# Weight narrowing in three separately emitted steps, outer products and token sums on GpSimd, and a new order of attention slots and loads, in a fused sketch-attention and gated-FFN kernel

## The chip, the cores and the metric

The kernel runs on one core of one Trainium2 chip. The metric is device time in microseconds (us). The core has five engines that run their own instruction streams: TensorE (PE, matmuls; its weight loads are shown as PEld), VectorE (DVE), ScalarE (ACT), GpSimd (POOL) and SyncE (SP, which here issues DMAs). They wait for one another through semaphores.

## The reference

Attention with a polynomial sketch: q and k are projected by two 8 x 32 sketches, and the outer product of the two projections (64 features) replaces the softmax kernel. Its output, laid out as 4352 tokens by 128, goes through a gated feed-forward layer. All in float32 for 4 batches, 4 heads, 1088 tokens, head width 32, and a hidden width of 1536:

```python
def phi(x):
    a = np.einsum('rd,bhsd->bhsr', S1, x)
    b = np.einsum('rd,bhsd->bhsr', S2, x)
    return np.einsum('bhsi,bhsj->bhsij', a, b).reshape(*x.shape[:-1], r * r)
q_p, k_p = (phi(q), phi(k))
kv = np.einsum('bhsf,bhsd->bhfd', k_p, v)
z = np.sum(k_p, axis=2)
num = np.einsum('bhsf,bhfd->bhsd', q_p, kv)
den = np.einsum('bhsf,bhf->bhs', q_p, z)[..., None] + 1e-06
attn = num / den
x = attn.transpose(0, 2, 1, 3).reshape(B * S, H * D)
gate = 1.0 / (1.0 + np.exp(-(x @ w_gate)))
return gate * (x @ w_val) @ w_out
```

The sketches and the three weight matrices arrive as float64 bits (pairs of 32-bit words), and the kernel turns them into float32 itself.

## The kernel before

**Feed-forward.** The 4352 tokens are cut into eight chunks of 512 and one of 256 (`tok_chk`). For each chunk there are 12 "waves", one for each 128-wide tile j of the hidden width (six in the last chunk, two tiles each). `w1` (from L287) issues a wave: two 128x512 matmuls into a `wave` PSUM tile (L300), a sigmoid on ACT (`sg`, L308), and a closure `glu` that multiplies value by gate on DVE (`g`, L313). `w2` (L252) accumulates `g` times the output weights into `moeout` (L258), two waves later. There are 102 waves.

**Attention.** For each batch: DVE transposes k (`turn_k`, tile `kT`, L356) and, in two chunks, q (`turn_q`, `qT`, L368). `kps` (L380) projects k, and DVE turns the result back (`kab`, L390). `outer` (L399) forms the products `kp` of one head. `kv` (L459) accumulates kp times v, and for batches 1 to 3 adds one matmul on `zs` (L471), the sum over tokens that `sum_z` (L493 to L497) makes of kp in four additions. `ab` (L422) projects q by both sketches into `aps` and `bps`; ACT copies aps to `asb` (L432) and DVE multiplies bps by it into `qp` (L441). Then `ndt` turns the copied kv (`kvd`, L482) on PE into `ndps`, from which DVE copies the denominators' weights `zb` (L514) and the numerators' weights `nd` (L516). `den` (L523) and its inversion (L534 to L541), `num` (L558) and the division into `xT` (L568) follow, for each q chunk. `xT` is what the waves read.

**The order.** Emission order sets the order on each engine; nothing reorders it. `slot(group, waves)` issues one attention group and then so many waves, so that PE always finds both kinds of work; the list of slots is written out by hand at the end of the function. PSUM has two `wave` tiles (shared by aps), one `two` tile (kps, bps, nps) and one `one` tile (kvz, ndps, dps), so a group can wait for the reader of the one before. dps takes the place of ndps and so waits for the copies of both zb and nd.

**Narrowing.** `narrow` turns a 128x3x128 tile of float64 bits, hidden tile j of all three matrices, into `w_sb`: `cap` (clamp of the high words, L94, DVE, reading every other word), two steps for `head` (L99, L103, DVE), `tail` (L107, ACT, low words), a square of cap (L108, ACT), an integer add of head and tail (L109, POOL), and the last step, a compare and multiply into `w_sb` (L113, DVE). During the first chunk wave j emits all but the last step for tile j+3 and then the last step of tile j+1, ahead of its matmuls. Tiles 0, 1 and 2 are narrowed ahead of the first wave. The pairs of tiles are loaded by `load_w`, four ahead.

**Loads.** SP issues all of them: the sketch rows, k and q of batch 0 in two halves each (288 and 256 KB), v, the first four weight pairs, then batch 1.

Of the kernel before, what the change touches and what calls it, by code (L numbers as in the profile page):

```python
# [14 lines left out]
MUL = ALU.mult  # L15
# [5 lines left out]
def kernel(  # L21
# [34 lines left out]
    sbN = ctx.enter_context(tc.tile_pool(name="sbN", bufs=4))  # L56
# [17 lines left out]
    q_chk = [(0, 9), (9, TP - 9)]  # L74
# [6 lines left out]
    def narrow(out, bits):  # L81
# [7 lines left out]
        def tmp(dt, tag):  # L89
            return sbN.tile([P, 3, P], dt, tag=tag, name=tag)[:, :n, :m]  # L90


        cap, head, tail = tmp(I32, "cap"), tmp(I32, "head"), tmp(I32, "tail")
        nc.vector.tensor_scalar(  # L94
            out=cap.bitcast(F32), in0=hi.bitcast(F32), scalar1=122880.0, scalar2=-122880.0,
            op0=ALU.min, op1=ALU.max,
        )

        nc.vector.tensor_scalar(  # L99
# [6 lines left out]

        nc.scalar.activation(out=tail, in_=lo, func=ACTF.Copy, scale=2.0**-29)  # L107
        nc.scalar.activation(out=cap.bitcast(F32), in_=cap.bitcast(F32), func=ACTF.Square)  # L108
        nc.gpsimd.tensor_tensor(out=head, in0=head, in1=tail, op=ALU.add)  # L109


        def last():
            nc.vector.scalar_tensor_tensor(  # L113
                out=out, in0=cap.bitcast(F32), scalar=1.265625 * 2.0**-30, in1=head.bitcast(F32),
                op0=ALU.is_ge, op1=MUL,
            )

        return last
# [49 lines left out]


    def load_rows(src, b, tag, parts=((0, T),)):  # L170
        t = ld.tile([P, T, D], F32, tag=tag, name=tag)
        for t0, t1 in parts:
            nc.sync.dma_start(
                out=t[:, t0:t1, :],
                in_=bass.AP(
                    tensor=src.tensor,
                    offset=src[b, 0].offset + t0 * D,
                    ap=[[T * D, P], [1, (t1 - t0) * D]],
                ),
            )  # L180
        return t
# [59 lines left out]

    zb = []
    for n in range(2):
        t = const.tile([P, H, 32], F32, tag=f"zb{n}", name=f"zb{n}")
        nc.gpsimd.memset(t, 0.0)
        zb.append(t)
# [40 lines left out]
    def w1():  # L287
# [107 lines left out]
    def outer(b, h, j0=0, j1=NJK):  # L395
# [3 lines left out]
        nc.vector.tensor_tensor(  # L399
# [89 lines left out]
    def sum_z(b):  # L489
# [3 lines left out]
        nc.vector.tensor_tensor(out=z4, in0=kp[:, :, 1:5], in1=kp[:, :, 5:9], op=ALU.add)  # L493
        nc.vector.tensor_tensor(out=z4[:, :, :2], in0=z4[:, :, :2], in1=z4[:, :, 2:], op=ALU.add)
        zs = sbA.tile([P, H, F], F32, tag="zs", name="zs")
        nc.vector.tensor_tensor(out=zs, in0=z4[:, :, 0], in1=z4[:, :, 1], op=ALU.add)
        nc.vector.tensor_tensor(out=zs[:64], in0=zs[:64], in1=kp[:64, :, 0], op=ALU.add)  # L497
        return zs

    def ndt(b):  # L500
# [15 lines left out]
        nc.vector.tensor_copy(out=ND[b], in_=ndps[:, 0, :P])  # L516
# [61 lines left out]
    turn_k(0, halves)  # L578
# [5 lines left out]
    for h in range(H):  # L584
        outer(0, h, 0, 5)
    kv(0, [1, 2, 3, 4])
    for h in range(H):
        outer(0, h, 5, NJK)
# [22 lines left out]
    turn_q(1, 0)  # L611
    slot(lambda: r_group((1, 0, 0), (0, 1, 1)), 1)
    slot(lambda: den(0, 1)(), 1)
    slot(lambda: num(0, 1)(), 1)
    turn_k(1)
    slot(lambda: kps(1), 1)

    for b in range(1, B):
        more = b + 1 < B

        few = b == 1
        load_batch(b + 1)
        if b == 1:
            for h in range(H):
                outer(b, h)
        turn_q(b, 1)
        slot(lambda: r_group((b, 1, 0), (b, 0, 0)), 1)
        zs = sum_z(b)
        slot(lambda: kv(b, [1, 2, 3, 4], zs), 1 if few else 2)
        slot(lambda: r_group((b, 0, 1), (b, 1, 0)), 1)  # L630
        turn_k(b + 1)
        slot(lambda: kv(b, [5, 6, 7, 8, 0], zs), 1 if few else 2)
        slot(lambda: r_group((b, 1, 1), (b, 0, 1)), 1)
        turn_q(b + 1, 0)
        if more:
            slot(lambda: kps(b + 1), 1 if few else 2)
            outer(b + 1, 0)
        slot(lambda: r_group((b + 1, 0, 0) if more else None, (b, 1, 1)), 1)
        if more:
            outer(b + 1, 1)  # L640
        slot(lambda: ndt(b), 1 if few else 2)
        if more:
            outer(b + 1, 2)
        slot(lambda: den(b, 0)(), 1 if few else 2)
# [7 lines left out]
        slot(num0_den1, 1)  # L652
        if more:
# [33 lines left out]
```

## Time and profile before

| | before |
|---|---|
| median of 3 runs | 342.51 us (342.16 to 343.34) |
| the profiled execution's own time | 344.44 us |
| its span, first to last instruction | 342.6 us |
| PE busy | 314.2 us (92%), mean granted clock 0.979 |
| DVE / ACT / POOL busy | 163.3 / 85.1 / 15.0 us |
| POOL instructions that do work | 21, of them 12 adds of 128x384 |

A row of the trace's timeline reads: start, length, engine, line of the kernel, operation, output tile and input tiles with shapes, the count of instructions, and in brackets how long the engine had been idle before it and what released it. Grouped rows read: busy time, mean in ns, and idle time before them by releaser. Rows of a stage give each engine's busy time, and the clock that PE was granted as a share of full speed. A wait that an engine that is not the bottleneck spends costs nothing.

### The profile page before, as it was taken

To read this page: it belongs to the slowest core of one execution; us is meant where nothing else is said; L and a number is where in the kernel's file an instruction comes from. 1 tells how busy PE (TensorE), PEld (TensorE's weight loads), DVE (VectorE), ACT (ScalarE), POOL (GpSimd) and SP (SyncE) were. 2 spreads that over 40 slices of the span, in tenths; PEclk is the share of its full clock that TensorE was granted. 3 is DMA by queue.
4 is the path that set the end of the run, shared out by engine and by line. 5 is a ranking of instruction groups with operands and counts; after the bars stand their busy time and mean duration, and the time that the engine had idled before them with its cause. 6 is when DMAs were issued, how large, how long until landed. Compare 5 with 4: busy or idle time off the path is not lost.

```text
span 342.6 us, 3915 instructions
## 1 busy us (share of the span) xinstructions
PE 314.2 (92%) x1552; PEld 137.8 (40%) x1552; DVE 163.3 (48%) x294; ACT 85.1 (25%) x152; POOL 15.0 (4%) x21
## 2 busy tenths in 40 slices
PE   1839878599999999999999999999999999999994
PEld 0512323133334434334443344444444444444682
DVE  3874798965675455475344432233233232322321
ACT  2143442123122222222222122222222222222220
POOL 1032131110000000000000000000000000000000
PEclk9995999989999999999999999999999999999999
DMA  6999302211100001000100010002001000100010
GB/s 166 303 316 310 65 0 68 65 35 36 31 2 1 2 16 17 0 0 2 31 2 0 0 32 2 0 0 32 0 0 25 7 0 0 32 0 0 2 31 15
DMA packets 25586, 14.08 MB, mean 41 GB/s; under 512 B 19168, under 2 KB 22752, under 8 KB 25568
## 3 DMA queue, kind: packets, MB, share of 16 engines
q1 hardware_dynamic: 25568, 13.83, 16.0%
q8 instruction: 12, 0.20, 0.2%
q14 instruction: 6, 0.05, 0.0%
HBM read 11.60 MB, written 2.23 MB: 40 GB/s over the span
## 4 chain that ended last, share of the span: by engine, by line
PE 83%; DVE 10%; DMA 2%; issue 2%; ACT 1%; SPq 1%; DVEq 0%
PE wave L300 49%; PE moeout L258 25%; PE aps L422 3%; PE kvz L459 2%; DMA q<-in_q_dram 2%; DVE g L313 1%; PE dps L523 1%; DVE head L103 1%; DVE cap L94 1%; PE nps L558 1%; DVE w_sb L113 1%; PE bps L422 1%; DVE head L99 1%; DVE kp L399 1%; DVE qT L368 1%
## 5 line engine op out<-in xcount | busy, mean ns | idle before, releaser
L300 PE MATMUL wave<-xT,w_sb 128*128 128x512 f32 (+1 forms) x432 | 195.7, 581 | 6.0 <-DVE w_sb L113 4.8
L313 DVE TENSOR_TENSOR g<-wave,sg 128x512 f32<-128x512 f32 x102 | 69.9, 685 | 122.7 <-ACT sg L308 122.7
L300 PEld LDWEIGHTS wave<-xT,w_sb 128*128 128x128 f32 x432 | 82.3, 193 | 103.4 <-issue 84.1
L308 ACT ACTIVATE sg<-wave 128x512 f32<-128x512 f32 x102 | 60.8, 596 | 204.3 <-PE wave L300 204.3
L258 PE MATMUL moeout<-g,w_sb 128*128 128x512 f32 (+1 forms) x216 | 107.4, 590 | 1.8 <-DVE g L313 1.8
L258 PEld LDWEIGHTS moeout<-g,w_sb 128*128 128x128 f32 x216 | 38.1, 191 | 44.1 <-issue 38.0
L441 DVE TENSOR_TENSOR qp<-bps,asb 128x576 f32<-128x576 f32 (+1 forms) x16 | 11.4, 720 | 22.9 <-PE bps L422 17.9
L422 PE MATMUL aps<-qT,s 32*64 32x288 f32 (+1 forms) x128 | 12.4, 468 | 5.0 <-DVE qT L368 2.8
L109 POOL TENSOR_TENSOR head<-head,tail 128x384 int32<-128x384 int32 (+1 forms) x13 | 14.1, 1089 | 55.3 <-DVE head L103 42.4
L108 ACT ACTIVATE cap<-cap 128x384 f32<-128x384 f32 (+1 forms) x13 | 6.5, 502 | 29.4 <-DVE head L103 29.4
L380 PE MATMUL kps<-kT,sk 64*32 64x288 f32 x64 | 3.9, 482 | 9.6 <-DVE kT L356 9.6
L399 DVE TENSOR_TENSOR kp<-kab 128x576 f32<-128x576 f32 (+2 forms) x20 | 12.5, 665 | 0.0
L422 PE MATMUL bps<-qT,s 32*64 32x288 f32 (+1 forms) x128 | 12.2, 451 | 0.0
L432 ACT COPY asb<-aps 128x576 f32<-128x576 f32 (+1 forms) x16 | 9.8, 610 | 8.0 <-PE aps L422 6.5
L422 PEld LDWEIGHTS aps<-qT,s 32*64 32x64 f32 x128 | 4.0, 147 | 18.2 <-issue 9.1
L568 DVE TENSOR_TENSOR xT<-nps,rb 128x576 f32<-128x576 f32 (+1 forms) x8 | 5.8, 724 | 7.7 <-PE nps L558 7.6
L459 PE MATMUL kvz<-kp,v 128*32 128x64 f32 (+1 forms) x288 | 8.8, 246 | 0.2 <-DVE kp L399 0.2
L459 PEld LDWEIGHTS kvz<-kp,v 128*32 128x32 f32 (+1 forms) x288 | 6.3, 124 | 6.2 <-issue 4.0
L103 DVE SCALAR_TENSOR_TENSOR head<-cap,head 128x384 int32<-128x384 int32 (+1 forms) x13 | 6.9, 533 | 0.5
L368 DVE STREAM_TRANSPOSE qT<-q 128x576 f32<-128x576 f32 (+1 forms) x8 | 5.9, 736 | 1.7 <-DMA q<-in_q_dram 1.7
L268 DVE STREAM_TRANSPOSE o_sb<-moeout 128x512 f32<-128x512 f32 (+1 forms) x9 | 6.1, 676 | 1.2 <-PE moeout L258 1.2
L107 ACT ACTIVATE tail<-w_in 128x384 int32<-128x384 uint32 x12 | 6.6, 553 | 0.0
(46 smaller groups left out, 87.1 us busy)
## 6 DMA issues: line engine op xcount, KB each, us to landing
v<-in_v_dram SPq DMA_DIRECT2D x16, 144.0 KB, 7.6
k<-in_k_dram SPq DMA_DIRECT2D x3, 544.0 KB, 7.0
q<-in_q_dram SPq DMA_DIRECT2D x3, 544.0 KB, 8.5
w_in<-in_moe_w_gate_dram SPq DMA_DIRECT2D x6, 256.0 KB, 5.6
w_in<-in_moe_w_val_dram SPq DMA_DIRECT2D x6, 256.0 KB, 5.6
w_in<-in_moe_w_out_dram SPq DMA_DIRECT2D x6, 256.0 KB, 5.7
out_dram<-o_sb SPq DMA_DIRECT2D x20, 64.0 KB, 2.0
k<-in_k_dram SPq DMA_DIRECT2D x1, 288.0 KB, 2.9
```

What stands on the lines that cost most here:

```text
L103: nc.vector.scalar_tensor_tensor(out=head, in0=cap, scalar=-0x40000000, in1=head, op0=ALU.bitwise_and, op1=ALU.bitwise_or)
L109: nc.gpsimd.tensor_tensor(out=head, in0=head, in1=tail, op=ALU.add)
L258: nc.tensor.matmul(out=moe["acc"][:, :tw], lhsT=w_sb[:, 2, j, :], rhs=g[:, jj, :tw], start=(j == 0), stop=(j == NJ - 1),)
L300: nc.tensor.matmul(out=wv[:, which, jj * tw : (jj + 1) * tw], lhsT=w_sb[:, which, j0 + jj, :], rhs=xT[:, t0 : t0 + tw], start=True, stop=True,
L308: nc.scalar.activation(out=sg, in_=wv[:, 0], func=ACTF.Sigmoid)
L313: nc.vector.tensor_tensor(out=g, in0=wv[:, 1], in1=sg, op=MUL)
L368: nc.vector.transpose(out=qT_of[b][:, t0 : t0 + tn].rearrange("p t c s -> p (t c s)"), in_=q_t[b][:, 2 * t0 : 2 * (t0 + tn)].rearrange("p ...
L399: nc.vector.tensor_tensor(out=KP[b][:, h, j0:j1].rearrange("p j (i l) -> p j i l", i=R), in0=bass.AP(tensor=a0.tensor, offset=a0.offset, a ...
L422: nc.tensor.matmul(out=dst[64 * c : 64 * c + 64, m, : 32 * tn], lhsT=sx[rows, :], rhs=qT_of[bb][rows, t0 : t0 + tn, c, :], start=True, sto ...
L432: nc.scalar.copy(out=ASB[a_of][:, :, :w], in_=aps[:, :, :w])
L441: nc.vector.tensor_tensor(out=QP[bb][:, 2 * pr : 2 * pr + 2, 32 * t0 : 32 * t0 + w], in0=bps[:, :, :w], in1=ASB[b_of][:, :, :w], op=MUL,)
L459: nc.tensor.matmul(out=kvz[32 * h : 32 * h + 32, F * which : F * which + F], lhsT=v_t[b][:kr, h, j, :] if which == 0 else ones[:kr, :], rh ...
```

## The change

- **Narrowing is a generator of three steps**, emitted apart: (0) cap and tail, with cap on POOL for the weights (on DVE for the sketches); (1) the two head steps, the square and the add; (2) the last step. Wave j emits step 0 of tile j+4, step 1 of tile j+2 and step 2 of tile j+1. Of the tiles ahead of the first wave, 0 gets all three steps, 1 two, 2 and 3 the first. `cap` has 5 buffers, `tail` 4, `head` 3 (4 each before).
- **Outer products go to POOL** for batches 1 to 3; for batch 0 one of four heads, in two pieces. The four additions of `sum_z` go to POOL. The copy of `nd` goes from DVE to ACT.
- **The q chunks** are 8 and 9 blocks (256 and 288 columns), 9 and 8 before.
- **Loads**: the first part of k (tokens for the first two kps groups) is requested by ACT; the second half of q comes behind v and the first weight pair.
- **Slots**: the two halves of kv become one group; a slot without a group stands ahead of kps of batch 1; the first aps of batch 1 has a slot of its own after it; `ndt` comes right behind kps; waves per slot are 1 in batch 1 and 2 in batches 2 and 3 throughout.

```diff
-    q_chk = [(0, 9), (9, TP - 9)]
+    q_chk = [(0, 8), (8, TP - 8)]
...
+        cap, tail = tmp(I32, "cap", 5), tmp(I32, "tail", 4)
+        eng.tensor_scalar(
             out=cap.bitcast(F32), in0=hi.bitcast(F32), scalar1=122880.0, scalar2=-122880.0,
             op0=ALU.min, op1=ALU.max,
         )
+        nc.scalar.activation(out=tail, in_=lo, func=ACTF.Copy, scale=2.0**-29)
+        yield
+
+        head = tmp(I32, "head", 3)
...
         nc.scalar.activation(out=cap.bitcast(F32), in_=cap.bitcast(F32), func=ACTF.Square)
         nc.gpsimd.tensor_tensor(out=head, in0=head, in1=tail, op=ALU.add)
+        yield
...
+    k_t[0] = load_rows(k, 0, "k", ((0, KBASE[2] + 1, nc.scalar), (KBASE[2] + 1, T, nc.sync)))
+    q_t[0] = load_rows(q, 0, "q", ((0, T0, nc.sync),))
     v_t[0] = load_v(0)
+    load_w(0)
+    load_rows(q, 0, "q", ((T0, T, nc.sync),), q_t[0])
...
         if ci == 0:
-            if j0 + 3 < NJ:
-                narrow_w(j0 + 3)
-            narrow_last(j0 + 1)
+            narrow_w(j0 + 4, 0)
+            narrow_w(j0 + 2, 1)
+            narrow_w(j0 + 1, 2)
...
-    def outer(b, h, j0=0, j1=NJK):
+    def outer(b, h, j0=0, j1=NJK, eng=nc.gpsimd):
...
-        nc.vector.tensor_tensor(
+        eng.tensor_tensor(
...
-        nc.vector.tensor_tensor(out=z4, in0=kp[:, :, 1:5], in1=kp[:, :, 5:9], op=ALU.add)
+        nc.gpsimd.tensor_tensor(out=z4, in0=kp[:, :, 1:5], in1=kp[:, :, 5:9], op=ALU.add)
...
-        nc.vector.tensor_copy(out=ND[b], in_=ndps[:, 0, :P])
+        nc.scalar.copy(out=ND[b], in_=ndps[:, 0, :P])
...
+    for j0, j1 in ((0, 5), (5, NJK)):
+        outer(0, 3, j0, j1)
+        for h in range(3):
+            outer(0, h, j0, j1, nc.vector)
...
     turn_k(1)
+    slot(None, 1)
     slot(lambda: kps(1), 1)
+    turn_q(1, 0)
+    outer(1, 0)
+    slot(lambda: r_group((1, 0, 0), None), 1)
+    outer(1, 1)
...
+        wn = 1 if b == 1 else 2
...
+        zs = sum_z(b)
+        slot(lambda: r_group((b, 1, 1), (b, 0, 1)), wn)
+        turn_k(b + 1)
+        slot(lambda: kv(b, [1, 2, 3, 4, 5, 6, 7, 8, 0], zs), wn)
+        if more:
+            slot(lambda: kps(b + 1), wn)
             for h in range(H):
+                outer(b + 1, h)
```

First place: DVE from the division of batch 0's first chunk (`xT`) to the weights of the first wave (`w_sb`). Before:

```order
L541 STREAM_TRANSPOSE rb<-rc 128x576
L568 TENSOR_TENSOR xT<-nps,rb 128x2x9x32
L94 TENSOR_SCALAR cap<-w_in 128x384
L99 TENSOR_SCALAR head<-cap 128x384
L103 SCALAR_TENSOR_TENSOR head<-cap,head 128x384
L113 SCALAR_TENSOR_TENSOR w_sb<-cap,head 128x3x128
```

and on the same engine in the changed kernel:

```order
L543 STREAM_TRANSPOSE rb<-rc 128x512
L570 TENSOR_TENSOR xT<-nps,rb 128x2x8x32
L114 SCALAR_TENSOR_TENSOR w_sb<-cap,head 128x3x128
L103 TENSOR_SCALAR head<-cap 128x384
L107 SCALAR_TENSOR_TENSOR head<-cap,head 128x384
L370 STREAM_TRANSPOSE qT<-q 128x576
```

The three steps of another tile no longer stand between xT and the first w_sb.

Second place: ACT from the copy of kv of batch 0 (`kvd`) on. Before, where `nd` was copied on DVE:

```order
L482 COPY kvd<-kvz 128x256
L107 ACTIVATE tail<-w_in 128x384
L108 ACTIVATE cap<-cap 128x384
L107 ACTIVATE tail<-w_in 128x384
L108 ACTIVATE cap<-cap 128x384
```

and now, with the copy of `nd`, which dps of batch 0 waits for:

```order
L484 COPY kvd<-kvz 128x256
L99 ACTIVATE tail<-w_in 128x384 x2
L110 ACTIVATE cap<-cap 128x384
L518 COPY nd<-ndps 128x128
L99 ACTIVATE tail<-w_in 128x384 x2
```

Two tails and a square stand between kvd and nd.

Third place: DVE from the return transposes of batch 1's k (`kab`) to the next q transpose (`qT`). Before:

```order
L390 STREAM_TRANSPOSE kab<-kps 128x288 x2
L313 TENSOR_TENSOR g<-wave,sg 128x512
L94 TENSOR_SCALAR cap<-w_in 128x384
L99 TENSOR_SCALAR head<-cap 128x384
L103 SCALAR_TENSOR_TENSOR head<-cap,head 128x384
L113 SCALAR_TENSOR_TENSOR w_sb<-cap,head 128x3x128
L399 TENSOR_TENSOR kp<-kab 128x576 x4
L368 STREAM_TRANSPOSE qT<-q 128x512
```

and in the changed kernel:

```order
L114 SCALAR_TENSOR_TENSOR w_sb<-cap,head 128x3x128
L392 STREAM_TRANSPOSE kab<-kps 128x288 x2
L315 TENSOR_TENSOR g<-wave,sg 128x512
L103 TENSOR_SCALAR head<-cap 128x384
L107 SCALAR_TENSOR_TENSOR head<-cap,head 128x384
L114 SCALAR_TENSOR_TENSOR w_sb<-cap,head 128x3x128
L370 STREAM_TRANSPOSE qT<-q 128x512
```

The cap and the four outer products have left DVE here. The outer products of batch 1 stand on POOL instead, among and behind the last two weight adds, with the sums of `sum_z` behind them:

```order
L401 TENSOR_TENSOR kp<-kab 128x576
L111 TENSOR_TENSOR head<-head,tail 128x384
L401 TENSOR_TENSOR kp<-kab 128x576 x2
L495 TENSOR_TENSOR z_653<-kp 128x1024
L496 TENSOR_TENSOR z_653<-z_653 128x4x128
L498 TENSOR_TENSOR zs<-z_653 128x256
L499 TENSOR_TENSOR zs<-zs,kp 64x256
```

Before, POOL had nothing here but the weight adds.

More of the change, by code (lines that the diff above doesn't have):

```diff
@@ L650, in num0_den1 @@
             invert()
-        slot(num0_den1, 1)
-        if more:
-            outer(b + 1, 3)
+        slot(num0_den1, wn)
         slot(lambda: num(b, 1)(), 1)
```

136 lines of the change are left out of this document (60 added, 76 removed).

## The prediction

> **What bounds the kernel now.** I read the clock and busy time by stage first, then who makes TensorE (PE) wait, then the startup in order of time, then the durations on VectorE (DVE) and GpSimd (POOL). The stages are cut where the granted clock changes; the columns are the stage, its length, the busy time (and instructions) of PE, PE's weight loads, DVE, ACT and POOL, the clock, the DMA share and GB/s:
>
> ```profile
> 0.00:24.89 24.89, 10.90 (x218) 6.01 (x218) 16.76 (x48) 6.79 (x16) 3.58 (x12) 0.99 0.91 262
> 24.89:34.48 9.59, 8.88 (x24) 2.98 (x32) 4.97 (x10) 3.38 (x8) 3.20 (x3) 0.50 1.05 300
> 34.48:50.00 15.52, 13.71 (x80) 4.60 (x65) 13.43 (x27) 6.45 (x13) 3.55 (x3) 1.00 0.16 34
> 50.00:60.00 10.00, 7.48 (x54) 2.67 (x56) 8.97 (x15) 3.44 (x7) 2.36 (x2) 1.00 0.20 58
> 60.00:68.61 8.61, 4.40 (x49) 1.67 (x49) 8.40 (x14) 1.45 (x3) 1.18 (x1) 1.00 0.20 65
> 68.61:72.02 3.41, 3.20 (x8) 1.10 (x5) 3.38 (x7) 1.48 (x3) 1.18 (x1) 0.50 0.00 0
> ...
> 80.50:338.20 257.70, 257.12 (x1059) 115.31 (x1058) 103.10 (x171) 59.97 (x101) 0.00 (x0) 1.00 0.05 9
> 338.20:342.60 4.40, 0.00 (x0) 0.00 (x0) 0.45 (x1) 0.00 (x0) 0.00 (x0) 0.90 0.18 30
> ```
>
> From 80.5 us on PE is idle for 257.70 - 257.12 = 0.58 us, and then 4.40 us at the end: that part is a fixed amount of matmul, and nothing that lightens DVE there is worth anything. What can be won lies before 80.5: the 24.89 us until the first wave; 9.46 us of PE idle after it (0.71, 1.81, 2.52, 4.21 and 0.21 by stage, none from 72.02 to 80.5); and two stretches at half clock, in which 8.88 and 3.20 us of matmul cost half their time, 6.0 us. Behind the idle time is DVE, 8.40 of 8.61 us busy where PE waits most:
>
> ```profile
> PE wave L300 <- DVE w_sb L113: 4.8, 2, 4.0
> PE kps L380 <- DVE kT L356: 2.5, 1, 2.5
> PE aps L422 <- DVE g L313: 2.2, 1, 2.2
> PE aps L422 <- DVE qT L368: 1.4, 1, 1.4
> PE moeout L258 <- DVE g L313: 1.2, 1, 1.2
> PE wave L300 <- ACT asb L432: 0.9, 2, 0.7
> ```
>
> These are PE's waits from 24.9 to 80.5 (total, times, longest); the 4.0 is the wait before the first wave itself. The rows that lead there:
>
> ```profile
> 3.20 0.91 SPq L173 DMA_DIRECT2D q<-in_q_dram  x2
> 9.32 0.78 DVE L368 STREAM_TRANSPOSE qT<-q 128x576 f32<-128x576 f32 x1 [1.67 <-DMA q<-in_q_dram]
> 10.24 1.50 PE L422 MATMUL aps<-qT,s 32*64 32x288 f32 x13 [1.36 <-DVE qT L368]
> 13.46 0.44 PE L459 MATMUL kvz<-kp,v 128*32 128x64 f32 x8
> 17.69 0.37 ACT L482 COPY kvd<-kvz 128x256 f32<-128x256 f32 x1 [4.54 <-PE kvz L459]
> 17.96 0.56 ACT L107 ACTIVATE tail<-w_in 128x384 int32<-128x384 uint32 x1
> 18.41 0.52 ACT L108 ACTIVATE cap<-cap 128x384 f32<-128x384 f32 x1
> 19.51 0.69 PE L523 MATMUL dps<-qp,zb 128*32 128x288 f32 x8 [0.90 <-DVE nd L516]
> 22.84 0.54 DVE L94 TENSOR_SCALAR cap<-w_in 128x384 f32<-128x384 f32 x1
> 24.29 0.55 DVE L113 SCALAR_TENSOR_TENSOR w_sb<-cap,head 128x384 f32<-128x384 f32 x1
> 24.90 3.78 PE L300 MATMUL wave<-xT,w_sb 128*128 128x512 f32 x4 [4.05 <-DVE w_sb L113]
> ```
>
> **Term 1, the first wave.** (a) DVE stood 1.67 us waiting for the first half of q, whose request SP issued behind two of k. One k request goes to ACT's queue, the half of q shrinks from 288 to 256 KB, and the second half moves behind v and the first weights. The landing is at best 1.67 earlier (then DVE is the bound) and at worst no earlier, since the same DMA engines move it; I take 0.9. (b) The aps and bps matmuls and the transpose shrink by 256/288: they fill PE from 10.24 to the first kvz matmul at 13.46, so 0.35 less, and 0.1 on the transpose. The outer products cannot bind kvz: one head moves to POOL and PE is busy with bps meanwhile. (c) The copy of nd goes to ACT, behind two tails and a square of the narrowing, and dps waits for it. kvd and the first tail start 0.27 apart, tail and square 0.45; three such steps put nd's start 0.27 + 3 x 0.45 = 1.6 after kvd's and its end, at under kvd's own 0.37, near 1.95; dps then stands 2.0 behind kvd against 19.51 - 17.69 = 1.82: a loss of 0.2. What stands behind nd on ACT (more tails) is wanted only later. (d) The division chain is 256 wide: 0.15 less. (e) Between xT and w_sb stood cap, head and head of tile 2; now the last step of tile 0 follows xT at once: 24.29 - 22.84 = 1.45 less. Sum: -0.9 - 0.45 + 0.2 - 0.15 - 1.45 = -2.75, the first wave at about 22.15; bounds -1.4 (no gain in the load, nd worse) and -3.6. On DVE the heads of tile 0 stand ahead of the zb copies, as the heads of two tiles did, but now wait through POOL's cap for the first weights. These have less ahead of them on the DMA engines than before, so I cost this at nothing; if they land so late that zb waits, dps waits as long. The request for k holds ACT before its first operation and the moved memsets, identity and zb lie on POOL and DVE, all while the sketch rows are still under way (POOL's first add waited 4.12 us): nothing.
>
> **Term 2, half clock.** Before both stretches PE had idled: 4.05 us ahead of 24.90, and 2.19 ahead of this row:
>
> ```profile
> 67.92 0.42 PE L422 MATMUL aps<-qT,s 32*64 32x256 f32 x1 [2.19 <-DVE g L313]
> 68.59 2.07 PE L258 MATMUL moeout<-g,w_sb 128*128 128x512 f32 x2
> ```
>
> So a gap of 2.2 us among thin work is enough for a lowered clock at 68.61, and the lowering lasts at least one stretch of 3.41 us. In the new order PE still idles some 2.5 us while the division chain runs on DVE. I keep one stretch like the first (8.8 us of matmul, 4.4 lost; bounds 1.7, one stretch of 3.41, and 6.0, as before). The second goes with the DVE work that caused it. Change: -1.6. The Trainium skill, "TensorE: Matmul & The Clock Gate", Part 1, says that the gate falls to half only after an idle window of about 3.4 us. By that rule the 2.5 us gap would not lower the clock, which is the first rival below; the trace differs, with its 2.19 us gap.
>
> **Term 3, PE idle after the first wave.** Means on DVE up to 80.5 us, two waves a slot apart, and POOL's rows, one with a collision:
>
> ```profile
> L313 DVE TENSOR_TENSOR g<-wave,sg 128x512 f32<-128x512 f32 x11 | 7.5, 678 | 3.3 <-ACT sg L308 3.3
> L103 DVE SCALAR_TENSOR_TENSOR head<-cap,head 128x384 int32<-128x384 int32 x12 | 6.7, 559 | 0.4
> L113 DVE SCALAR_TENSOR_TENSOR w_sb<-cap,head 128x384 f32<-128x384 f32 x12 | 6.6, 551 | 0.0
> L99 DVE TENSOR_SCALAR head<-cap 128x384 int32<-128x384 int32 x12 | 4.3, 360 | 0.4
> L399 DVE TENSOR_TENSOR kp<-kab 128x576 f32<-128x576 f32 x4 | 3.6, 948 | 0.0
> L390 DVE STREAM_TRANSPOSE kab<-kps 128x288 f32<-128x288 f32 x4 | 1.7, 452 | 1.0 <-PE kps L380 1.0
> ```
>
> ```profile
> 40.77 1.88 PE L300 MATMUL wave<-xT,w_sb 128*128 128x512 f32 x4
> 44.11 1.88 PE L300 MATMUL wave<-xT,w_sb 128*128 128x512 f32 x4
> ```
>
> ```profile
> 4.56 0.32 POOL L109 TENSOR_TENSOR head<-head,tail 128x64 int32<-128x64 int32 x1 [4.12 <-DVE head L103]
> 18.60 1.96 POOL L109 TENSOR_TENSOR head<-head,tail 128x384 int32<-128x384 int32 x2 [12.92 <-ACT tail L107]
> 63.36 1.18 POOL L109 TENSOR_TENSOR head<-head,tail 128x384 int32<-128x384 int32 x1 [6.07 <-DVE head L103]
> 63.60 2.02 DVE L493 TENSOR_TENSOR z<-kp 128x1024 f32<-128x1024 f32 x1
> 103.13 1.21 DVE L493 TENSOR_TENSOR z<-kp 128x1024 f32<-128x1024 f32 x1
> ```
>
> A wave costs DVE 0.54 + 0.36 + 0.56 + 0.55 + 0.68 = 2.69 us before and 2.15 after; with some 0.7 of attention that is below a PE slot of about 3.3 (44.11 - 40.77 = 3.34, with a den group between and no wait). Batch 1 also loses on DVE its four outer products (3.6) and the sums (2.0 for the first of four). So the waits for g (2.2 and 1.2), w_sb (0.8), the small ones (0.4) and kT (2.5, now with a slot free of attention ahead of it) go. What is late next: wave 1 still waits for the asb copy, 0.7. Behind kps of batch 1 DVE has w_sb, two kab, g, head, head, w_sb and qT before the next aps, 0.5 + 0.85 + 0.65 + 0.9 + 0.5 + 0.7 = 4.1 (each means above, less what neighbours overlap), while PE has moeout and a wave, a slot without its attention, 2.7: 1.4 idle, in the place of the old 1.4. The second qT: 0.7 by the same count. Together 2.8. For collisions with POOL I add 1.7: a sum of 1.21 us took 2.02 beside POOL's 1.18, so two-input work on the two engines partly excludes each other, and cap, add and outer products now run on POOL. Idle: 4.5 in place of 9.46, -5.0; bounds 2.8 (no collisions) and 8.5 (collisions as in the second rival, 5.7).
>
> POOL's own time: (1.96/2 - 0.32)/320 = 2.07 ns an element over a base of 0.19 gives an estimate of 1.4 us for an outer product and 5.0 for the four sums of a batch; cap lies between 0.54 (DVE) and 1.18 (POOL's add of the same size), midway 0.85. A wave needs 0.85 + 1.18 = 2.0 there, under the slot. In batch 1 the last two outer products and the sums, 2.8 + 5.0 = 7.8 us, follow the add of the last tile. That add comes behind DVE's qp, g and two heads after wave 8, some 4 us; PE reaches the matmul on zs three slots of 3.4 and the kvz steps later, some 12 to 13: 8 to 9 us for 7.8, about 0.5 to spare. In batches 2 and 3 nine slots, 30 us, lie between kps and kvz. The second chunk of q, now 288 wide instead of 256, adds 0.2 to PE's work behind the first wave. Other wave counts per slot change no matmul, and the loads that move on SP are ones that no engine waits for in the view above.
>
> **Sum**: -2.75 - 1.6 - 5.0 + 0.2 = -9.15. The profiled execution took 344.44 us around its span of 342.6, 1.9 above the median of the three runs, 342.51; as a difference the sum holds for either: 335.3 profiled, 342.5 - 9.15 = 333.4 in the median.
>
> **Rivals.** First, the clock stays high or recovers after one stretch: for it speaks that the gap shrinks from 4.05 to 2.5; against it the 2.19. Up to 4.4 less is lost, of which DVE gives back about 1: 330. Second, the collisions make DVE the bound again: its two-input and scalar steps, 0.56 + 0.55 + 0.36, and POOL's 2.0 add to 3.5 a wave, above 3.34; if they exclude each other wholly, DVE's 2.15 + 0.7 with 0.9 of waiting comes to 3.75, 0.4 above the slot in ten waves: 4 more, 337.5. For it speaks the 2.02; against it that w_sb, beside the start of POOL's add, kept its 551 ns. The Trainium skill, "GPSIMD Engine Reference", section 1, has the SBUF interfaces shared in just these cases, two SBUF inputs or a two-port mode; the trace agrees at 63.60. Third, the other side: POOL's broadcast products or strided cap are much dearer than its integer add. Then zs holds up kvz of batch 1, and PE stands. With 0.5 to spare and 9.15 to lose, the 7.8 us must take 17.4, 2.2 times the estimate; at 3 times, 7.8 x 2 - 0.5 = 15.1 is lost and the time is 348. No row shows a broadcast product on POOL; against it, the add's rate is that of two reads and one write as well.
>
> **How the numbers follow.** Forecast 0.55, first rival 0.20, second 0.15, third 0.06, and 0.04 that terms cancel within 0.3% (1 us, about what a measurement can tell from no change). Faster 0.90, same 0.04, slower 0.06. The range, 328.5 to 338.5, holds the first two rivals and the bounds of the terms where they do not all fall together.
>
> **What would show it.** Right: the first wave near 22; one stretch at 0.50; kps of batch 1 by 49 (52.28 before) and its kvz done near 70, PE dense behind it; outer products on POOL near 1.4 us. Wrong: dps more than 2.5 us behind kvd; a PE wait of several us on zs; DVE's heads or w_sb well above 0.56; a second stretch at half clock.

## The result, and the profile after

The changed kernel takes 329.46 us (median of 4 runs, 328.98 to 330.88) against 342.34 for the kernel before (4 runs, 340.15 to 343.34): a ratio of 0.964, 95% interval 0.958 to 0.970, 12.9 us faster. The forecast was 333.4, 9.15 faster. The profiled execution took 329.06 us around a span of 327.3.

The stages of the changed kernel, cut at the first wave, where the clock comes back (24.66), and then by time (columns as in the prediction). The first stage has half clock too, from 17.84 on:

```profile
0.00:21.06 21.06, 9.52 (x218) 4.37 (x218) 13.62 (x38) 6.39 (x15) 6.47 (x16) 0.92 0.93 297
21.06:24.66 3.60, 3.59 (x4) 1.18 (x4) 3.39 (x6) 1.49 (x3) 2.04 (x3) 0.50 1.07 248
24.66:35.00 10.34, 9.58 (x49) 3.36 (x49) 6.76 (x14) 5.36 (x11) 4.51 (x6) 1.00 0.92 266
35.00:50.00 15.00, 14.15 (x75) 5.50 (x75) 14.51 (x29) 7.43 (x15) 8.92 (x10) 1.00 0.13 41
50.00:60.00 10.00, 9.21 (x58) 3.32 (x64) 6.32 (x12) 3.45 (x8) 6.90 (x6) 1.00 0.16 57
60.00:65.76 5.76, 5.76 (x104) 2.73 (x92) 3.27 (x4) 2.16 (x4) 4.13 (x4) 1.00 0.02 6
65.76:323.00 257.24, 255.76 (x1057) 114.69 (x1055) 92.77 (x153) 60.16 (x103) 19.40 (x16) 1.00 0.06 11
```

TensorE is dense from 60 us on (80.5 before). VectorE is still nearly full from 35 to 50, 14.51 of 15, but nowhere behind that. TensorE's waits from 20 to 80 us, all of them:

```profile
PE wave L302 <- DVE w_sb L114: 2.0, 1, 2.0
PE aps L424 <- DVE qT L370: 1.6, 2, 0.9
PE wave L302 <- ACT asb L434: 0.8, 1, 0.8
```

The 2.0 is the wait ahead of the first wave; kT, g, moeout and the later w_sb are gone. The startup in order of time, the rows that answer to those of before:

```profile
4.41 0.20 DVE L95 TENSOR_SCALAR cap<-sr_in 128x64 f32<-128x64 f32 x1 [3.06 <-DMA sr_in<-in_S_dram]
9.06 1.14 PE L424 MATMUL aps<-qT,s 32*64 32x256 f32 x10
15.47 0.37 ACT L484 COPY kvd<-kvz 128x256 f32<-128x256 f32 x1 [3.56 <-PE kvz L461]
16.38 0.34 DVE L516 COPY zb<-ndps 64x4 f32<-64x4 f32 x2 [0.41 <-PE ndps L505]
17.35 0.66 PE L525 MATMUL dps<-qp,zb 128*32 128x256 f32 x8 [1.01 <-ACT nd L518]
19.85 0.69 DVE L570 TENSOR_TENSOR xT<-nps,rb 128x512 f32<-128x512 f32 x1
20.46 0.55 DVE L114 SCALAR_TENSOR_TENSOR w_sb<-cap,head 128x384 f32<-128x384 f32 x1
21.07 3.75 PE L302 MATMUL wave<-xT,w_sb 128*128 128x512 f32 x4 [2.03 <-DVE w_sb L114]
24.86 0.60 ACT L310 ACTIVATE sg<-wave 128x512 f32<-128x512 f32 x1 [0.20 <-PE wave L302]
26.23 1.12 PE L302 MATMUL wave<-xT,w_sb 128*128 128x512 f32 x2 [0.76 <-ACT asb L434]
```

Where the 15.3 us between the two spans went, by the prediction's terms. "Lost" is matmul time under half clock, half of each such stretch's busy time:

| | before | after | change | forecast |
|---|---|---|---|---|
| first wave | 24.90 | 21.07 | -3.83 | -2.75 |
| lost to half clock behind it | 6.04 | 1.80 | -4.24 | -1.6 |
| TensorE idle from the first wave to 80 us | 9.46 | 2.40 | -7.06 | -5.0 |
| idle from 80 us to the last matmul | 0.55 | 1.28 | +0.73 | 0 |
| matmul time at full clock, and the end | | | -0.9 | +0.2 |

The +0.73 is one wait of a wave for asb, at 147.56, which the kernel before does not have. The medians differ by 12.9 only: the profiled execution of before was 2.1 us above its median, that of the changed kernel 0.4 below. Of the 2.1, the run of before with filled gaps (below) accounts for 0.7 in the startup; the rest stays open.

### The profile page after: what moved, and what is told of

Its sections match the earlier page's. It is cut to its first block, busy times and chain, and to the rows that moved or that the text cites. A ratio compares the mean times of both kernels' runs of the same rounds, so it can differ in the third digit from the quotient of the medians.

```text
span 327.3 us, 3936 instructions
## 1 busy us (share of the span) xinstructions
PE 307.6 (94%) x1552; PEld 135.1 (41%) x1552; DVE 140.9 (43%) x252; ACT 86.4 (26%) x156; POOL 52.4 (16%) x59
## 4 chain that ended last, share of the span: by engine, by line
PE 87%; DVE 6%; DMA 3%; SPq 1%; ACT 1%; issue 1%; DVEq 0%; ACTq 0%
PE wave L302 52%; PE moeout L260 27%; PE aps L424 2%; DMA w_in<-in_moe_w_out_dram 2%; PE dps L525 2%; DMA w_in<-in_moe_w_val_dram 1%; PE kvz L461 1%; PE nps L560 1%; DVE g L315 1%; DVE w_sb L114 1%; DVE head L107 1%; PE bps L424 1%; SPq L188 1%; DVE rb L543 0%; DVE head L103 0%
## 5 line engine op out<-in xcount | busy, mean ns | idle before, releaser
L302 PE MATMUL wave<-xT,w_sb 128*128 128x512 f32 (+1 forms) x432 | 193.2, 574 | 3.5 <-DVE w_sb L114 2.0
L401 POOL TENSOR_TENSOR kp<-kab 128x576 f32<-128x576 f32 (+2 forms) x14 | 15.5, 1133 | 43.6 <-DVE kab L392 43.6
L443 DVE TENSOR_TENSOR qp<-bps,asb 128x512 f32<-128x512 f32 (+1 forms) x16 | 11.5, 722 | 23.3 <-PE bps L424 17.7
L424 PE MATMUL aps<-qT,s 32*64 32x256 f32 (+1 forms) x128 | 12.1, 443 | 1.6 <-DVE qT L370 1.6
L434 ACT COPY asb<-aps 128x512 f32<-128x512 f32 (+1 forms) x16 | 9.8, 612 | 7.0 <-PE aps L424 5.4
L424 PE MATMUL bps<-qT,s 32*64 32x256 f32 (+1 forms) x128 | 11.4, 425 | 0.0
L570 DVE TENSOR_TENSOR xT<-nps,rb 128x512 f32<-128x512 f32 (+1 forms) x8 | 5.8, 724 | 10.6 <-PE nps L560 10.4
L461 PE MATMUL kvz<-kp,v 128*32 128x64 f32 (+1 forms) x288 | 7.0, 222 | 0.7 <-DVE kp L401 0.6
L495 POOL TENSOR_TENSOR z<-kp 128x1024 f32<-128x1024 f32 x3 | 7.4, 2476 | 0.2
L536 DVE STREAM_TRANSPOSE dT<-dps 128x256 f32<-128x256 f32 (+1 forms) x8 | 3.7, 463 | 7.5 <-PE dps L525 7.5
```

The source lines that it names most:

```text
L302: nc.tensor.matmul(out=wv[:, which, jj * tw : (jj + 1) * tw], lhsT=w_sb[:, which, j0 + jj, :], rhs=xT[:, t0 : t0 + tw], start=True, stop=True,
L401: eng.tensor_tensor(out=KP[b][:, h, j0:j1].rearrange("p j (i l) -> p j i l", i=R), in0=bass.AP(tensor=a0.tensor, offset=a0.offset, ap=[pst ...
L424: nc.tensor.matmul(out=dst[64 * c : 64 * c + 64, m, : 32 * tn], lhsT=sx[rows, :], rhs=qT_of[bb][rows, t0 : t0 + tn, c, :], start=True, sto ...
L434: nc.scalar.copy(out=ASB[a_of][:, :, :w], in_=aps[:, :, :w])
L443: nc.vector.tensor_tensor(out=QP[bb][:, 2 * pr : 2 * pr + 2, 32 * t0 : 32 * t0 + w], in0=bps[:, :, :w], in1=ASB[b_of][:, :, :w], op=MUL,)
L461: nc.tensor.matmul(out=kvz[32 * h : 32 * h + 32, F * which : F * which + F], lhsT=v_t[b][:kr, h, j, :] if which == 0 else ones[:kr, :], rh ...
```

## The experiments

All are the changed kernel with an edit, but one; all compute the same. Each set of four ran on one chip beside runs of the kernel before (medians 343.45, 342.20 and 343.04 us), so ratios to before are given as well. My theory was the sum of the prediction: VectorE is what TensorE waits for, and half clock follows from TensorE's idle time.

**The yardstick**, unchanged.

> The changed kernel as it is, as the yardstick for the others: 329.5 us, 0.962 of the kernel before. If its second profile shows again one stretch at half clock of about 6.8 us around the first wave and 2.4 us of TensorE idle up to 66 us, these belong to the kernel; if the stretch is missing or longer, the half-clock loss varies from execution to execution and explains the spread of 329.0 to 330.9.

330.03 us (329.45 to 330.70), ratio 0.963 (0.957 to 0.970). The first wave at 21.46, half clock for 6.8 us from 18.2 to 25.1, TensorE idle 2.40 us to 80: in both traces the pattern is the same, so it belongs to the kernel.

**Products and sums on VectorE.**

```diff
-    def outer(b, h, j0=0, j1=NJK, eng=nc.gpsimd):
+    def outer(b, h, j0=0, j1=NJK, eng=nc.vector):
...
-        nc.gpsimd.tensor_tensor(out=z4, in0=kp[:, :, 1:5], in1=kp[:, :, 5:9], op=ALU.add)
...
+        nc.vector.tensor_tensor(out=z4, in0=kp[:, :, 1:5], in1=kp[:, :, 5:9], op=ALU.add)
...
```

> The changed kernel with the outer products and token sums of batches 1 to 3 on VectorE again (the one head of batch 0 stays on GpSimd). Theory (the move to GpSimd frees the engine that TensorE waits for): some 6 us of batch 1's work, 4 x 0.95 + about 2.2, return to VectorE between 45 and 65 us, where it has 2.4 to 3.4 of 3.41 us busy up to 52 us and about 5 us free behind that; TensorE idles 1.5 to 2.5 us more, 331.5 us. Rival (the new order of the slots alone removes the waits; GpSimd only costs by collisions): no change or faster, 329.0 to 329.5 us, with VectorE's head steps back at 0.56 us instead of 0.96.

336.52 us, ratio 0.982 (0.976 to 0.989): 6.5 slower than the yardstick, over three times what I expected. TensorE's idle time to 80 us went from 2.40 to 5.59, and one wait had a sequel:

```profile
59.50 0.45 PE L424 MATMUL aps<-qT,s 32*64 32x288 f32 x1 [2.26 <-DVE qT L370]
```

```profile
57.50:60.92 3.42, 1.42 (x18) 0.54 (x18) 2.42 (x3) 1.02 (x2) 0.64 (x1) 1.00 0.13 27
60.92:64.33 3.41, 3.41 (x5) 1.30 (x4) 3.34 (x6) 0.05 (x1) 0.00 (x0) 0.50 0.35 137
```

Behind the stretch that holds the 2.26 us gap stands another stretch at half clock. The lost time grew by 2.1 us, idle by 3.2 (and 0.3 behind 80 us), and 1.0 came with a later first wave, which the edit does not touch. The theory's direction holds; it had left out that each wait can cost a half-clock stretch as well.

**First loads as before.**

```diff
-    k_t[0] = load_rows(k, 0, "k", ((0, KBASE[2] + 1, nc.scalar), (KBASE[2] + 1, T, nc.sync)))
-    q_t[0] = load_rows(q, 0, "q", ((0, T0, nc.sync),))
+    k_t[0] = load_rows(k, 0, "k", ((0, KBASE[2] + 1, nc.sync), (KBASE[2] + 1, T, nc.sync)))
+    q_t[0] = load_rows(q, 0, "q", ((0, T0, nc.sync), (T0, T, nc.sync)))
...
-    load_w(0)
-    load_rows(q, 0, "q", ((T0, T, nc.sync),), q_t[0])
...
```

> The changed kernel with the first loads in the order of before: both parts of k and both of q on SyncE, then v, then the weights. Theory (the load order carries about half of the earlier first wave): VectorE waits for q again, the first aps goes from 9.1 to about 10.3 and the first wave from 21.1 to 22.5 or 23, 331.0 us. Rival (the earlier start comes from the last narrowing step and the shorter first chunk; the transfers share their engines whatever the order): the first wave stays within 0.4 us of 21.1, 329.5 to 329.9 us.

330.74 us (330.17 to 333.77), ratio 0.967 (0.959 to 0.975): no difference that these runs resolve. The rows that decide it:

```profile
3.65 0.20 DVE L95 TENSOR_SCALAR cap<-sr_in 128x64 f32<-128x64 f32 x1 [2.30 <-DMA sr_in<-in_S_dram]
8.04 0.71 DVE L368 STREAM_TRANSPOSE qT<-q 128x512 f32<-128x512 f32 x1 [0.91 <-DMA q<-in_q_dram]
8.90 1.45 PE L422 MATMUL aps<-qT,s 32*64 32x256 f32 x13 [0.53 <-DVE qT L368]
```

VectorE waits for q again, 0.91 us, but the sketch rows, with k's first request behind theirs and not beside it (issued at 2.10 instead of 0.73), are in by 3.65 instead of 4.41, and the first aps stands at 8.90, earlier than in any run with the new load order (9.06 to 9.47). The load order moves a wait from q to the sketch rows and is worth nothing; my theory's aps at 10.3 was wrong. The rival had the time and not the first wave, which came at 22.07: kvz started at 12.59, 3.7 us behind aps in place of 2.5. Of that, 0.73 us is a wait for VectorE's products (kp); the rest stays open.

**Narrowing emitted as before**, cap on VectorE.

```diff
-                narrowing[j] = narrow(w_sb[:, :, j, :], w_in[n][:, :, jj], nc.gpsimd)
+                narrowing[j] = narrow(w_sb[:, :, j, :], w_in[n][:, :, jj], nc.vector)
...
-            narrow_w(j0 + 4, 0)
-            narrow_w(j0 + 2, 1)
+            narrow_w(j0 + 3, 0)
+            narrow_w(j0 + 3, 1)
             narrow_w(j0 + 1, 2)
...
+    narrow_w(2, 0)
+    narrow_w(2, 1)
     narrow_w(0, 2)
-    narrow_w(1, 1)
```

> The changed kernel with the narrowing emitted as before: cap on VectorE, cap to add of a tile in one piece, the last step of tile 0 behind cap and head of tile 2. Theory (the order brought 1.5 us ahead of the first wave, and cap on GpSimd relieves a VectorE that is 14.5 of 15 us busy from 35 to 50 us): the first wave at 22.6, a wave costs VectorE 0.54 us more, about as long as a slot, and TensorE waits 1 to 3 us more: 333 us (331.5 to 335). Rival (cap is hidden wherever it runs; only the place of the last step counts): 331.0 us, with TensorE's waits up to 66 us unchanged at 2.4.

340.26 us (10 runs, 338.47 to 341.38), ratio 0.992 (0.988 to 0.995): 10.2 of the 12.9 us are gone. In the trace, of an execution of 341.38 us and so 1.1 above the median, the first wave is at 24.35, of which xT to wave takes 2.66 us against 1.21. Most of the rest is clock; the last two rows are one of two later stretches, at 67.8, and what stands ahead of it (the other is at 57.6):

```profile
19.99:33.64 13.65, 9.19 (x32) 2.65 (x16) 9.08 (x19) 3.70 (x7) 3.54 (x3) 0.50 0.96 258
...
64.43:67.84 3.41, 1.53 (x19) 0.39 (x18) 2.54 (x2) 0.60 (x1) 3.25 (x3) 1.00 0.00 0
67.84:71.25 3.41, 3.41 (x5) 1.35 (x6) 1.75 (x3) 0.64 (x1) 1.09 (x2) 0.50 0.49 163
```

Lost to half clock: 7.7 us against 1.8, in this execution; five of the ten, 338.47 to 339.51 us long, were granted 0.972 to 0.976 on the mean against 0.967 here, so they may have lost less. The run takes back the order of the steps and cap's engine together, so what each is worth by itself is not shown. Undoing this part costs 10.2 and undoing the products 6.5, together more than the whole change brought: either one puts VectorE back in front of TensorE, and the second then adds less.

**Slots as before, products and sums on VectorE.** The list of slots of before, over the last but one edit.

```diff
-    slot(None, 1)
-    slot(lambda: kps(1), 1)
-    turn_q(1, 0)
+    slot(lambda: kps(1), 1)
...
-        slot(lambda: kv(b, [1, 2, 3, 4, 5, 6, 7, 8, 0], zs), wn)
+        slot(lambda: kv(b, [1, 2, 3, 4], zs), 1 if few else 2)
...
+        slot(lambda: kv(b, [5, 6, 7, 8, 0], zs), 1 if few else 2)
```

> The changed kernel with products and sums on VectorE, as in the run with 336.5 us, and the attention steps in the slots of before (one wave in half of the slots, the kvz products in two pieces, the outer products of batch 1 in one piece). Theory (the slot order is worth something by itself: it spreads the transposes and products over slots with room): the waits of before for kT and g come back, 338.5 us (337.5 to 339.5). Rival (the order only serves GpSimd's later sums and brings nothing while VectorE makes them): 336.0 to 337.0 us.

335.61 us, ratio 0.983 (0.977 to 0.988) beside 0.982 for the new slots with products on VectorE. In the trace, of an execution of 338.35 us and so 2.7 above the median, the waits for kT (1.6) and g (2.2, 1.2) did come back, others went. The times are the same within these intervals, of about 2 us each way: the rival was right, and the runs show no gain of the slot order by itself. Whether GpSimd could serve the old order was not tried; nor were the widths of the q chunks by themselves.

**More matmuls in the gaps.** Three runs put 128x256 matmuls without a use where TensorE idles in the startup: two between nps and the first wave; these and one ahead of ndps and two ahead of dps; and in the kernel before, one, two and seven at the same places. The edit of the second:

```diff
+    def fill(n):
...
+            nc.tensor.matmul(
+                out=t[:, i % 2, :256], lhsT=ident, rhs=kT_of[0][:, :256], start=True, stop=True
+            )
...
+    fill(1)
     ndt(0)
+    fill(2)
...
     divide = num(0, 0)
+    fill(2)
     invert()
```

> The changed kernel with two matmuls of 128 x 256 more (about 0.43 us each at full clock, their result is not used) between nps of batch 0 and the first wave, where TensorE idles 2.0 us. Theory (the clock of a stretch of 3.41 us goes by how busy TensorE was in the stretch before): the stretch that ends near the first wave is now busier, the next one is at full clock, the first wave takes 1.9 us in place of 3.75, and the time is 328.2 us, 1.8 below 330.0. Rival (once lowered, the clock returns only after a stretch that is busy throughout): still 6.8 us at half clock, 330.0 us.

329.28 us, ratio 0.962 (0.957 to 0.967), between the two. The trace is the rival's: the clock fell at 18.8, ahead of the two matmuls, which ran at half speed, and half clock lasted 6.8 us as in the yardstick. The other three executions, 0.2 to 0.7 us shorter, were granted 0.992 to 0.996 on the mean instead of 0.987, so their half clock may have been shorter; no trace shows them.

> The changed kernel with five such matmuls: one between kvz and ndps, two between ndps and dps, two between nps and the first wave. Theory (as above): TensorE is busy for over 2.5 us of each 3.41, no stretch is at half clock, 328.0 us. Rival (the lowering does not come from TensorE's own idle time in these stretches, but from what the other engines and the transfers do): the clock drops near 18 us all the same, the five matmuls cost 0.4 to 0.9 us each, and the time is 330.0 to 331.5 us.

329.26 us, ratio 0.963 (0.958 to 0.967). The mechanism came, the gain did not. In the trace, of the longest of the four executions (330.45), the startup ran at full clock and the first wave took 1.96 us; but the next wave hardly moved, and half clock came later instead:

```profile
21.44 1.96 PE L302 MATMUL wave<-xT,w_sb 128*128 128x512 f32 x4 [0.54 <-DVE w_sb L114]
24.43 0.52 ACT L110 ACTIVATE cap<-cap 128x384 f32<-128x384 f32 x1 [1.21 <-DVE head L107]
24.86 0.58 ACT L310 ACTIVATE sg<-wave 128x512 f32<-128x512 f32 x1
26.02 2.50 PE L302 MATMUL wave<-xT,w_sb 128*128 128x512 f32 x4 [1.97 <-ACT asb L434]
```

```profile
23.94:27.35 3.41, 1.44 (x7) 0.68 (x4) 2.71 (x6) 2.29 (x5) 1.80 (x3) 1.00 0.99 309
27.35:30.76 3.41, 3.41 (x20) 0.94 (x19) 0.98 (x3) 1.78 (x4) 1.48 (x2) 0.50 0.91 310
```

The first sigmoid starts at 24.86 as in the changed kernel, because ScalarE has the square of tile 2 ahead of it, and that waits for VectorE's head of tile 2 (its releaser in the row of 24.43). TensorE then idles 1.97 us, and a half-clock stretch follows. The other three executions took 328.90 to 329.59 us and were granted 0.996 to 0.998 on the mean, against 0.993 here, so they may not have had that stretch.

> The kernel before with ten such matmuls in its startup: one ahead of ndps, two ahead of dps, seven in the 4.05 us ahead of the first wave; their result is not used. Theory (half of what the changed kernel wins is half clock that follows from TensorE's idle time): the three stretches at half clock around the first wave vanish, 4.4 us of lost matmul time come back, of which VectorE, nearly always busy from 34 to 68 us, takes about 1.5 back: 340.5 us against 343.5. Rival (the lost clock is hidden behind VectorE anyway): 343 to 344 us.

339.87 us (9 runs), ratio 0.994 (0.990 to 0.997): 2.3 faster than before. The three stretches around the first wave vanished, and so did the one at 68.6; one came at 48.2, behind a stretch with 0.93 us of matmul. 4.3 us of lost time came back (6.0 to 1.7), and about half of that shows in the whole time. This run also shows the startup of before in another execution, with nothing changed up to kvd:

```profile
15.65 0.37 ACT L482 COPY kvd<-kvz 128x256 f32<-128x256 f32 x1 [3.44 <-PE kvz L459]
16.08 0.44 PE L503 MATMUL ndps<-ident,kvd 128*128 128x128 f32 x2
16.73 1.26 DVE L103 SCALAR_TENSOR_TENSOR head<-cap,head 128x384 int32<-128x384 int32 x1
17.91 0.33 DVE L514 COPY zb<-ndps 64x4 f32<-64x4 f32 x2
```

kvd is 2.0 us earlier than in the profiled execution of before (17.69), but VectorE takes most of that back: zb starts 1.4 us after ndps has ended (16.08 + 0.44), behind the heads of two tiles, only 0.8 earlier than there (18.72), and the first wave (24.17) only 0.7 earlier.

**Sums twice.** GpSimd's first two sums of each batch are made a second time.

```diff
+        nc.gpsimd.tensor_tensor(out=z4, in0=kp[:, :, 1:5], in1=kp[:, :, 5:9], op=ALU.add)
+        nc.gpsimd.tensor_tensor(out=z4[:, :, :2], in0=z4[:, :, :2], in1=z4[:, :, 2:], op=ALU.add)
         zs = sbA.tile([P, H, F], F32, tag="zs", name="zs")
```

> The changed kernel with the first two of GpSimd's four sums of each batch made twice, about 3.9 us more per batch; the result is the same. Theory (in batch 1 the sums end only 0.2 us before TensorE takes them, at 64.4 us): TensorE waits 3.7 us at the products with the sums of batch 1 and nowhere else, and as that is a gap longer than the 2.2 us of before, one stretch at half clock follows: 335.2 us (333.5 without the stretch). Rival (GpSimd has slots to spare, since later steps of TensorE can go ahead): 330 us.

335.46 us, ratio 0.979 (0.973 to 0.985). GpSimd and TensorE in batch 1, and the two stretches behind:

```profile
67.64 0.72 POOL L501 TENSOR_TENSOR zs<-zs,kp 64x256 f32<-64x256 f32 x1
68.41 0.32 PE L473 MATMUL kvz<-zs,ones 128*32 128x64 f32 x8 [3.58 <-POOL zs L501]
```

```profile
65.77:69.18 3.41, 0.77 (x9) 0.45 (x10) 0.00 (x0) 0.37 (x1) 2.43 (x3) 1.00 0.66 172
69.18:72.60 3.42, 3.42 (x6) 1.31 (x4) 0.00 (x0) 0.00 (x0) 0.00 (x0) 0.50 0.00 1
```

Of 3.9 us more on GpSimd TensorE waits 3.6, at this place only, and pays 1.7 more at half clock, as the theory said: 5.3 of 5.4 measured.

**The sigmoid ahead in ScalarE's queue**, alone and with the five matmuls.

```diff
-            narrow_w(j0 + 4, 0)
-            narrow_w(j0 + 2, 1)
-            narrow_w(j0 + 1, 2)
+            narrow_w(j0 + 2, 1)
+            narrow_w(j0 + 1, 3)
...
         nc.scalar.activation(out=sg, in_=wv[:, 0], func=ACTF.Sigmoid)
+        if ci == 0:
+            narrow_w(j0 + 4, 0)
+            narrow_w(j0 + 2, 2)
```

The square is a step of its own here (2), and the last step is 3.

> The changed kernel with tail and square of the narrowing of later tiles emitted behind the sigmoid of the wave on ScalarE, not ahead of it. Theory (the first sigmoid starts at 24.86 whether the first wave runs at full or half clock, since ScalarE's square ahead of it waits for VectorE's head of tile 2; the half clock under the first wave is hidden by that): the sigmoid moves to the middle of the first wave, about 23.3, the gate product ends when the second half of the wave allows it, wave 1 starts 0.4 to 0.7 us earlier, 329.4 us. Rival (the asb copy, which ends at the same time, holds wave 1 by itself): 330.0 us.

331.09 us, ratio 0.965 (0.961 to 0.970): no gain. A sigmoid starts at the end of its wave, not in the middle as I expected, so under half clock the wave itself holds it.

> The last one with the five matmuls that keep the clock up until the first wave. Theory (with the sigmoid out of the queue the full clock is worth something): sigmoid at 22.5, gate product at about 24.8, wave 1 at 25.4 in place of 26.0 to 26.6; TensorE's gap ahead of it shrinks from 2.0 to 1.4 us. If the half-clock stretch behind that gap goes too: 327.3 us; if it stays: 329.0. Rival (transfers of the weights set the pace of these waves, not the clock and not the queue): 329.3 to 330 us, with wave 2 where it was.

329.42 us, ratio 0.961 (0.956 to 0.966). Both causes removed:

```profile
21.51 1.95 PE L302 MATMUL wave<-xT,w_sb 128*128 128x512 f32 x4 [0.38 <-DVE w_sb L115]
23.50 0.60 ACT L310 ACTIVATE sg<-wave 128x512 f32<-128x512 f32 x1 [0.66 <-PE wave L302]
25.31 1.98 PE L302 MATMUL wave<-xT,w_sb 128*128 128x512 f32 x4 [1.20 <-DVE g L318]
```

From the first wave to the second it is 5.16 us in the changed kernel, 5.19 with the sigmoid moved, 4.58 with full clock, and 3.80 with both, and no stretch of this run is at half clock. The two causes ended at the same time and hid each other. The 327.3 us that I expected without half clock did not come; in the whole time the gain is at most a microsecond: against the yardstick's trace, half clock gives 1.8 back, TensorE idles 0.6 more and its matmuls take 0.5 more.

**All of it**, with nd on VectorE and the two transposes of q each a step earlier.

```diff
+    turn_q(1, 0)
     slot(lambda: kps(1), 1)
-    turn_q(1, 0)
...
     outer(1, 1)
+    turn_q(1, 1)
```

> All that seemed worth something: the last one, the copy of nd on VectorE again, and the two transposes of q of batch 1 each one step earlier. Theory (VectorE has room one step earlier at both places): the two waits for qT, 0.85 and 0.79 us, go, nd wins 0.1 to 0.3: 1.7 us below the run before it, 325.6 to 327.3 us. Rival (in the stage from 35 to 50 us VectorE is 14.5 of 15 us busy, so the first transpose only pushes the wait on to the gate product or w_sb): 0.8 us below it.

328.53 us (328.36 to 329.12), ratio 0.958 (0.954 to 0.963). Three of its four times lie below all eight of the changed kernel; the intervals overlap, so it is faster by about 1 us with some doubt, and 0.9 below the run before it, about what the rival had. Both waits for qT are gone; of the 1.6 us, 0.7 came back where GpSimd had no slack, a wait that the changed kernel does not have:

```profile
PE kvz L476 <- POOL zs L502: 0.7, 1, 0.7
```

## Why the prediction was right, and where it was off

**The class and the chain of reasons held**: VectorE's load in the first 80 us, given to GpSimd and ordered later, is what TensorE had waited for. The three parts of the time were each too small or right by luck.

**Term 1** (-2.75; -3.83 in the traces). (e), no tile between xT and w_sb, is right: 24.29 - 22.17 = 2.12 became 20.46 - 19.85 = 0.61, -1.51 for -1.45. (c) is right: dps stands 1.88 behind kvd, 2.0 forecast. (a), the landing of q for -0.9, is worth nothing: the run with the old loads has its first aps at 8.90. The profiled execution of before was merely late: with the same loads the filled kernel before has its first aps at 9.30 instead of 10.24. What I passed over stands in its place: "on DVE the heads of tile 0 stand ahead of the zb copies, as the heads of two tiles did" was costed at nothing, but two caps and two pairs of heads held zb 1.4 us in the filled kernel before, and one pair holds nothing now, since zb (16.38) follows ndps at once. Against the startup of the filled kernel before (first wave 24.17) the yardstick's 21.46 is 2.7 earlier: the sum came out right by luck, one part of it wrong and another missing.

(b) has a wrong step too, "the outer products cannot bind kvz". On VectorE six products beside GpSimd's two and its caps took longer than eight had before, and TensorE waited for them:

```profile
10.75 3.00 DVE L399 TENSOR_TENSOR kp<-kab 128x320 f32<-128x320 f32 x8
9.97 3.93 DVE L401 TENSOR_TENSOR kp<-kab 128x320 f32<-128x320 f32 x6
PE kvz L461 <- DVE kp L401: 0.6, 2, 0.3
```

The first row is of the kernel before, the other two of the changed one; the yardstick has the same 0.6 us.

**Term 2** (-1.6; -4.24) is the largest miss, a wrong step: "I keep one stretch like the first (8.8 us of matmul)" assumed that the lowering begins at the first wave. It began at 17.9 and ended within 0.2 us of the end of that wave:

```profile
14.43:17.84 3.41, 1.90 (x69) 1.08 (x58) 1.83 (x6) 2.37 (x7) 1.46 (x2) 1.00 1.09 382
17.84:21.25 3.41, 1.38 (x21) 0.41 (x18) 2.99 (x7) 0.37 (x1) 0.55 (x2) 0.50 1.05 321
21.25:24.66 3.41, 3.41 (x4) 0.99 (x4) 3.20 (x6) 1.49 (x3) 2.04 (x3) 0.50 1.06 253
```

Half of the lowered time fell into startup work that VectorE hides, and 3.59 us of matmul under it lost 1.80. The first rival (330) thus had the right size. That the second stretch goes with the DVE work was right.

**Term 3** (idle 4.5; 2.40 came). The wait for asb was 0.76 for 0.7; the two for qT 0.85 and 0.79 for 1.4 and 0.7. The mis-sized part is the 1.7 for collisions: behind the first wave none reached TensorE. They took place on VectorE, in head 0.96 us beside a product for the usual 0.35:

```profile
48.78 1.18 POOL L401 TENSOR_TENSOR kp<-kab 128x576 f32<-128x576 f32 x1
49.21 0.96 DVE L103 TENSOR_SCALAR head<-cap 128x384 int32<-128x384 int32 x1
...
58.80 2.59 POOL L495 TENSOR_TENSOR z<-kp 128x1024 f32<-128x1024 f32 x1
61.47 1.27 POOL L496 TENSOR_TENSOR z<-z 128x512 f32<-128x512 f32 x1
62.82 0.73 POOL L498 TENSOR_TENSOR zs<-z 128x256 f32<-128x256 f32 x1
63.63 0.73 POOL L499 TENSOR_TENSOR zs<-zs,kp 64x256 f32<-64x256 f32 x1
64.55 0.32 PE L473 MATMUL kvz<-zs,ones 128*32 128x64 f32 x8
```

but from 50 to 60 us VectorE has only 6.32 of 10 us to do. TensorE's one wait there, the 0.79 for qT, has no such step ahead of it: VectorE was idle for 1.76 us after the slow head and before the steps that lead to qT. So the second rival failed.

**GpSimd's prices** were near: a product 1.18 for 1.4, the four sums 5.3 for 5.0, cap 0.53 for 0.85. The sums end at 64.36 and TensorE takes them at 64.55: 0.2 us to spare for "about 0.5". The third rival had the right place and not the price; the run with longer sums shows it to within 0.3 us.

**The clock's rule.** I argued from the length of the gap, 2.19 us. That was the wrong measure: in the kernel before a gap of 2.48 us (kT) lowered nothing, in the run with five matmuls one of 1.97 did. The last section has what fits.

## What to carry to other kernels

A wait of TensorE has two prices, itself and the half-clock stretch that it may bring on; count both, and count what already hides the second. Two causes that end at the same time hide each other: take away both before calling either harmless. When work goes to a helper engine, write down how late its result is against its reader; here 0.2 us was left, and in the last run a gain of 1.6 us ahead of it lost 0.7 to that.

## What the runs showed of the hardware

**The clock goes by stretches of 3.41 us.** Twelve of the fourteen traces have half clock between 8 and 90 us, and each time it lasts a whole number of them: 3.4, 6.8, 10.2 or 13.65 us. I cut the traces from 8 to 90 us on each one's raster and counted matmul time at half clock half. Of 25 stretches with under 1.55 us of it (45%), 24 were followed by half clock; one (1.41) was not. Above that only the startup stretch with the end of the small kvz products was, eight times at 1.88 to 1.92 us, while the same place in the kernel before, 1.93, was not, and neither were stretches of 1.67 to 1.84 elsewhere; why these eight were stays open. A stretch at half clock counts 1.71 at most, so only a nearly full one, 3.2 us busy or more, ended the lowering; 3.0 did not. So the place of a gap on the raster counts: the one of 2.48 us lay across two stretches, in which 1.67 and 2.66 us of matmul were left. The Trainium skill, "TensorE: Matmul & The Clock Gate", Part 1, has a free-running window of 3413 ns, and half rate after an idle window. The raster agrees; here up to 1.5 us of matmul in a window did not keep the clock up.

**The same small matmuls take different times.** From the first kvz matmul to kvd it was 4.23 us in the profiled execution of before and 3.15 in the filled one, with the same instructions; in the runs of the changed kernel it was 3.32 to 4.37 (the changed kernel's own 3.87 has the wait of 0.6 for kp in it). This moves the first wave by up to 1 us between executions. What decides it stays open.

**Two-input work on GpSimd stretches VectorE's.** Beside a product on GpSimd a head step took 0.96 us instead of 0.35 (above), and in the last run a w_sb 1.53 instead of 0.55. The Trainium skill, "GPSIMD Engine Reference", section 1, names two SBUF inputs as a case in which the two engines share their interfaces; w_sb has two. The head step that was stretched reads one; the same line names a 2-port performance mode as the other case, and no run here shows whether head ran in it.
